# Moving a conversion, three chunks and an output step round the first join of a one-core delta-rule and hard-swish kernel

## The chip, the cores and the metric

The kernel runs on one core of a Trainium2 chip. The metric is the device time of one execution in microseconds (us). The kernel before takes 664.41 us, the median of 3 runs (663.94 to 665.17). A profiled execution of it took 662.06 us, with a span of 660.3 us from its first to its last instruction.

A core has five instruction queues that run side by side and wait for each other by semaphores: PE (matrix multiplication, into PSUM), VectorE (DVE), ScalarE (ACT), GpSimd (POOL) and SyncE (SP), which here issues the loads and stores. Each queue runs its instructions in the order in which the program has them. An instruction that waits holds all that stand behind it on its queue.

## The reference

Two blocks, one behind the other. The first is the delta rule, for 4 batches and 8 heads, 768 steps in time and 48 values a head; the second is a hard-swish MLP on 3072 tokens (384 to 2048 to 384).

```python
k_n = k / (norm(k) + 1e-06)
for t in range(S):
    y[:, :, t] = einsum('bhd,bhde->bhe', q[:, :, t], state)
    v_old = einsum('bhde,bhd->bhe', state, k_n[:, :, t])
    state = state + bt * einsum('bhd,bhe->bhde', k_n[:, :, t], v[:, :, t] - v_old)
...
h = x @ w_in
g = h * clip(h + 3.0, 0.0, 6.0) / 6.0
out = g @ w_out
```

`x` is `y` with its heads put side by side: 3072 rows of 384.

## The kernel before

**Time in chunks.** The 768 steps are cut into N = 24 chunks of C = 32, numbered t. Within a chunk the recurrence is a triangular system of 32 by 32 for each batch and head. `prep` (L505) makes keys, their transposes (`pt`, L524) and the products of keys with keys and queries (`sc`, L547), masked into L and LB (L558). The chunks are inverted in groups: group 0 is chunk 0 alone, group 1 is chunks 1 to 4. `halves_of` (L715) inverts the two 16 by 16 halves of every system of group 1 at once on VectorE: a transpose (L469), then 28 dependent steps that alternate between a product (L730) and a subtraction (L735), a memset (L740) and a transpose back (L473). `join` (L666) puts the halves of one chunk together: a memset on POOL (L691), a transpose on VectorE (L694), a product on PE (`pi`, L684), an addition and a transpose on VectorE (L698, L702), a second product `pi`, and a copy into X on ScalarE (L710). The first join is that of chunk 1.

**The chain.** `chain(t)` (L787) carries the state from chunk to chunk: `ks` (L806) from the state, R on VectorE (L901, L909), `pz` (L827) from X and R, a copy Z on ScalarE (L927), `su` (L938) and the new state (L956). Beside it runs the output of the chunk: `py` (L827's helper, from Z and LB), y (L861 on ScalarE for chunk 0, L843, L819 and L863 for the others), the transposes `yt` (L873) and the copy xT (L877), from which the MLP starts.

**The MLP.** Two chunks make a block of 256 tokens. For block 0, `up(0, 0)` and `up(0, 1)` (L982) run the first matrix for one chunk of tokens each, in 16 pieces of 128 hidden columns, called chunks of `ph` here: three matmuls (L994, 6 records in the trace), a relu on ScalarE (L1001) and a VectorE instruction (L1004) that writes g and frees the PSUM bank. Banks come from a ring of four (`NPM`), which `py`, `yt`, `pi`, `pz` and `pt` use too; a new user takes the bank whose last reader stands earliest in the order, and waits for that reader.

**The weights.** The two matrices come in 16 pieces in a form that has to be converted: four *scale steps* a piece on ScalarE (L356), which write one of two buffers `es[i % 2]` in turn, and three *conversion steps* on VectorE (L378, L383, L389), of which the last reads that buffer and writes the matrix:

```python
d, z = raws[i], like(es[i % 2], i)
...
out=weights[i][0], in0=mf, scalar=2.0**-20, in1=like(es[i % 2], i).bitcast(BF16),
```

Pieces are counted from 0 in the code: the seventh is i = 6, the ninth i = 8, and both use `es[0]`.

**The order.** The first part of the program is written out by hand: the text `ORDER` is read word by word, and each word records the next step of one generator, `*n` times. Behind it a plan goes on by slots. The words that matter here:

- `a`: a scale step. `c`: a conversion step. `w`, `k`, `q`, `v`: one load of weights, keys, queries or values, issued by SP
- `y0`: the steps of the output of chunk 0 (`py`, y, `yt`, xT). `h1`: the steps of chain 1
- `i1`: the steps of `halves_of` for group 1. `x1`, `x2`: the steps of the joins of chunks 1 and 2. `n5`: the norms of keys of chunk 5 (L407 on ScalarE, L413 on VectorE)
- `ua`: the matmuls of one chunk of `ph` of `up(0, 0)`. `ra`: its relu. `ga`: its L1004

Of the kernel before, what the change touches and what calls it, by code (L numbers as in the profile page):

```python
# [23 lines left out]
m0 a n2 m1 p0 x0*2 w q x0 n1 x0*3 c*2 n2 a k s p1*2 a s*2 k q s*2 x0 n2 k*2 c x0 n2 x0 w q a*4 q p1  # L24
n2 k*2 a x0 m2 p1 c*2 p1 n2*3 b1 q b0 s p1 x0 q w x0 n2 q*2 c*3 x0 n4 k p1 k p2*2 x0*2 a*2 c a*2 q*3
a*2 w v p3*2 q x0 q n4 p2*2 c p2 v c n4*2 a*3 z v n4 c a m3 v c p2 n4*2 q p2 k c b2 h0 c h0 w a*2 h0
p4*2 a*2 m4 p3 q*4 h0 q k w p4*2 c*5 v*2 p3 k p3*3 k*2 p4*2 v*2 p4 m6 k a w a w i1*3 k i1*7 a i1*2 a
i1*2 v i1*2 k b3 k y0 c y0*3 ua*2 ra*2 i1*3 w v ga v a*3 i1*2 ua i1 h1 i1 q w ua ra ua i1 ra*2 ga i1
k ua a*2 ra ga i1 ga ua ra ua ra i1 ga i1*4 ua ga n5 x1*2 k x1 c a ra v a*2 ga x2 k*2 ga*2 ua*2 x1
ra*2 x1*2 ua h1*2 n5 k ga c ra ga*2 h1 c y1*2 ua ra w ga ua ra x2 n5 ga y1*2 ua ra ga h1 v*3 n5*2 k  # L30
y1*2 ua a ra x2 ub*2 a n5 rb*2 h1 x3 ga c*2 v W a h2 y2 gb ub rb gb x2 gb ub*2 n5*2 b4 rb n5 x2*2 h2
gb rb gb m5 a n5*2 y2 ub rb gb v c q*2 v q*5 n5 ub n5 rb gb h2 c h2 q ub y2 h2 y2 rb ub p5 b5 rb
gb*2 a*2 x3 p5 ub y2*2 k p5*2 h2 rb h3 p5 gb h3 ub*2 q rb gb rb gb ub a x3 p6 v c x4 x3 rb gb ub p7
rb gb y3 c*2 v c p7*2 y3 v p7*2 b6 x3 q x3 ub p6 h3 a p6 c p5*2 rb gb k m7 w p6 h3 u p6 k*2 q*3 a*2
y3 a p6 c y3 v y3*2 u n9 v k q a c a c*2 u*2 ru gu w k a*2 c a*2 x4 c*2 ru p7 a gu k u a*2 p7 p6 m8
u*3 a k u*2 k h3 w ru*2 a*2 gu*2 x4 c*2 x4 k c*2 a p8 k a*2 u ru k h3 u*2 h4 ru a b8 gu k gu y4 p8*3
u h4 k*2 c q k*9 q u p8*2 x4 k ru k*2 gu k c n9 q u q*2 p8 k*2 b7 n9*2 i2 u x4 q i2*2 q ub ru gu u
rb gb i2*2 h4*2 u*2 i2 ru i2*6 y4 i2 gu i2*7 u i2 ru gu i2 u*3 ru i2*4 gu ru i2*2 v i2 c gu u*3 a u
ru c i2 u*2 i2 gu i2*3 q i2*5 y4 h4 n9 i2 e*2 n9*2 i2*4 q i2 y4 e n9 u ru i2*3 u i2 ru*2 gu h4 u n9
i2*2 u i2 e i2*6 y4 u k n9*3 u gu i2 y4 n9 i2 p9 q i2*2 gu  # L40
"""


# [1521 lines left out]
```

## Time and profile before

| what | value |
|---|---|
| median of 3 runs | 664.41 us |
| the profiled execution | 662.06 us |
| its span | 660.3 us |
| PE busy, 0 to 45 us | 24.69 us |
| PE busy, 47.5 to 61.24 us | 9.81 of 13.74 us |
| VectorE busy, 47.5 to 61.24 us | 12.95 of 13.74 us |
| ScalarE busy, 47.5 to 61.24 us | 10.62 of 13.74 us |
| PE busy, 61.24 to 140 us | 78.76 of 78.76 us |
| PE idle before `yt` of chunk 0, for y (L861) | 2.41 us |
| PE idle before the first `ph`, for xT (L877) | 0.58 us |
| PE idle before the first `pi` of the join | 0.94 us |

Times in the views are in us from the start of the span. In the timeline a line has start, length, engine, line of the code, operation, what is written and read, and how often; idle time before it stands in square brackets. In the table by stretches a line has the stretch, its length, busy time of PE, of PE's weight loads, VectorE, ScalarE and POOL with the number of instructions, then PE's granted clock as a share of full speed, the mean share of the DMA engines, and GB/s. The profile's lines for dependent VectorE instructions overlap at their ends by a little.

### The profile page before, as it was taken

How to read it: one execution, taken by the hardware profiler on the slowest of the kernel's cores; microseconds unless marked ns; L12 is line 12 of the kernel's file. 1: busy time of each engine (PE TensorE's matmuls, PEld its weight loads, DVE VectorE, ACT ScalarE, POOL GpSimd, SP SyncE). 2: the span in 40 equal slices, each digit the busy share in tenths (PEclk: the TensorE clock that was granted, in tenths of full speed). 3: DMA queues.
4: the chain of work that ended last, by engine and by line, in shares of the span. 5: the costliest groups of instructions: out<-in, count | busy, mean ns of one | idle time of the engine just before them, and what ended most of it. 6: DMA issues, size and time to landing. Idle time of an engine off the chain costs nothing.

```text
span 660.3 us, 26640 instructions
## 1 busy us (share of the span) xinstructions
PE 632.5 (96%) x11640; PEld 569.2 (86%) x11640; DVE 499.2 (76%) x1170; ACT 282.3 (43%) x548; POOL 225.1 (34%) x352
## 2 busy tenths in 40 slices
PE   2768999999999999999999999999999999999997
PEld 2658987776689989999999999999999999999997
DVE  5899877798657988758988848979658998456354
ACT  5887689332243154154154244244244144153250
POOL 6531022003661353553254354164051242331430
PEclk9998999999999999999999999999999999999999
DMA  7888346202040030041030030020020020000000
GB/s 174 204 198 235 77 102 164 51 25 43 9 87 18 3 74 3 3 90 22 3 74 3 2 74 3 2 63 2 3 50 2 3 49 3 23 18 2 26 1 24
DMA packets 88692, 33.28 MB, mean 50 GB/s; under 512 B 80224, under 2 KB 83424, under 8 KB 88576
## 3 DMA queue, kind: packets, MB, share of 16 engines
q1 hardware_dynamic: 88224, 31.29, 20.8%
q8 instruction: 91, 1.49, 0.9%
q10 hardware_dynamic: 352, 0.30, 0.2%
q14 instruction: 25, 0.20, 0.1%
HBM read 26.84 MB, written 4.72 MB: 48 GB/s over the span
## 4 chain that ended last, share of the span: by engine, by line
PE 91%; DVE 3%; DMA 2%; SPq 1%; ACT 1%; issue 1%; DVEq 0%
PE po L1226 28%; PE ph L1066 27%; PE ph L994 9%; PE po L1162 6%; PE ks L806 4%; PE su L938 3%; PE pt L524 3%; PE pz L827 3%; PE py L827 3%; PE sc L547 2%; PE yt L873 1%; DMA spare<-in_moe_w_in_dram 1%; PE pi L684 1%; DMA w_out<-in_moe_w_in_dram 1%; SPq L168 1%
## 5 line engine op out<-in xcount | busy, mean ns | idle before, releaser
L1066 PE MATMUL ph<-xT,w_in 128*128 128x128 f32 (+1 forms) x720 | 156.8, 321 | 0.0
L1030 POOL TENSOR_TENSOR g<-g 128x256 f32<-128x256 f32 (+1 forms) x144 | 88.6, 616 | 104.7 <-ACT g L1080 99.1
L1066 PEld LDWEIGHTS ph<-xT,w_in 128*128 128x128 f32 x720 | 116.8, 191 | 6.7
L1226 PE MATMUL po<-w_out,g 128*128 128x192 f32 x640 | 110.6, 326 | 0.0
L1226 PEld LDWEIGHTS po<-w_out,g 128*128 128x128 f32 x640 | 104.6, 190 | 0.5
L1080 ACT ACTIVATE g<-ph 128x512 f32<-128x512 f32 x72 | 43.1, 598 | 105.1 <-PE ph L1066 105.1
L1226 PE MATMUL po<-spare,g 128*128 128x192 f32 x480 | 86.7, 332 | 0.0
L1226 PEld LDWEIGHTS po<-spare,g 128*128 128x128 f32 x480 | 77.2, 190 | 1.8
L994 PE MATMUL ph<-xT,w_in 128*128 128x128 f32 (+1 forms) x384 | 72.0, 338 | 0.6 <-ACT xT L877 0.6
L1236 POOL TENSOR_TENSOR o<-o,u 128x192 f32<-128x192 f32 x18 | 13.3, 739 | 163.8 <-ACT o L1233 86.6
L994 PEld LDWEIGHTS ph<-xT,w_in 128*128 128x128 f32 x384 | 59.6, 195 | 7.7 <-ACT xT L877 0.8
L1093 DVE TENSOR_TENSOR g<-ph,g 128x256 f32<-128x256 f32 x72 | 30.2, 419 | 46.8 <-PE ph L1066 33.5
L759 DVE TENSOR_TENSOR pr<-A 128x30 f32<-128x30 f32 (+9 forms) x150 | 57.3, 382 | 3.3
L1212 DVE TENSOR_TENSOR g<-g 128x512 f32<-128x512 f32 x80 | 56.1, 722 | 3.5 <-PE po L1226 3.5
L1113 DVE SCALAR_TENSOR_TENSOR g<-o,g 128x512 f32<-128x512 f32 x72 | 52.6, 730 | 7.8 <-ACT o L1110 7.7
L764 DVE TENSOR_TENSOR A<-A,pr 128x30 f32<-128x30 f32 (+9 forms) x150 | 55.1, 367 | 3.3
L1110 ACT ACTIVATE o<-g,halves 128x512 f32<-128x512 f32 x72 | 52.2, 725 | 11.3 <-DVE g L1113 8.4
L1066 PE MATMUL ph<-beta_tok,sums_in 128*128 128x128 f32 x288 | 55.9, 275 | 0.0
L356 ACT ACTIVATE spare<-spare,places 128x768 uint16<-128x768 uint16 (+1 forms) x56 | 52.8, 947 | 3.2 <-DMA kf<-in_k_dram 1.6
L1233 ACT ACTIVATE o<-po 128x192 f32<-128x192 f32 x40 | 13.3, 332 | 82.7 <-PE po L1226 79.2
L510 POOL TENSOR_TENSOR kb<-kf,inv 128x384 f32<-128x384 f32 x24 | 21.7, 907 | 75.5 <-issue 43.1
L1162 PE MATMUL po<-w_out,g 128*128 128x384 f32 x128 | 45.4, 490 | 0.0
(141 smaller groups left out, 1019.1 us busy)
## 6 DMA issues: line engine op xcount, KB each, us to landing
kf<-in_k_dram SPq DMA_DIRECT2D x96, 48.0 KB, 2.6
qb<-in_q_dram SPq DMA_DIRECT2D x96, 48.0 KB, 2.4
vf<-in_v_dram SPq DMA_DIRECT2D x96, 48.0 KB, 2.1
out_dram<-o SPq DMA_DIRECT2D x90, 48.0 KB, 1.6
spare<-in_moe_w_in_dram SPq DMA_DIRECT2D x4, 768.0 KB, 6.6
w_out<-in_moe_w_in_dram SPq DMA_DIRECT2D x4, 768.0 KB, 6.1
w_out<-in_moe_w_out_dram SPq DMA_DIRECT2D x4, 768.0 KB, 5.8
spare<-in_moe_w_out_dram SPq DMA_DIRECT2D x4, 768.0 KB, 5.2
```

The source lines that it names most:

```text
L356: nc.scalar.activation(out=z, in_=z if n else d.bitcast(I16)[:, :, :, 3], func=func, bias=places[:, n : n + 1], scale=scale,)
L759: nc.vector.tensor_tensor(out=pv, in0=A[:, j + 1 :, j].unsqueeze(2).to_broadcast([n, w, j]), in1=A[:, j, 0:j].unsqueeze(1).to_broadcast([n ...
L764: nc.vector.tensor_tensor(out=A[:, j + 1 :, 0:j], in0=A[:, j + 1 :, 0:j], in1=pv, op=ALU.subtract)
L994: nc.tensor.matmul(ph[:, cols], lhsT=w_in[:, s, f * 128 : (f + 1) * 128], rhs=xT[:, s, cols], start=(s == 0), stop=(s == NKT - 1),)
L1030: nc.gpsimd.tensor_tensor(out=out, in0=a, in1=b, op=op)
L1066: nc.tensor.matmul(ph[:, n], lhsT=w, rhs=x, start=start, stop=stop, skip_group_check=True)
L1080: nc.scalar.activation(out=gt, in_=ph[:], func=ACTF.Copy)
L1110: nc.scalar.activation(out=r, in_=g, func=ACTF.Relu, bias=half, scale=1.0 / 6.0)
L1113: nc.vector.scalar_tensor_tensor(out=g, in0=r, scalar=1.0, in1=g, op0=ALU.min, op1=ALU.mult)
L1162: nc.tensor.matmul(pos[c][:], lhsT=gs[blk, f // 2][:, f % 2, c * P : (c + 1) * P], rhs=w_out[:, f, :], start=(f == 0), stop=(f == NFC - 1),)
L1212: nc.vector.tensor_tensor(out=A(f, *out, 4), in0=A(f, *a, 4), in1=A(f, *b, 4), op=op)
L1226: nc.tensor.matmul(ps[n][:], lhsT=A(f - f % 2, *a)[:, f % 2], rhs=b[:, f], start=(f == 0), stop=(f == HF - 1),)
```

## The change

Only the text `ORDER` changes. The words are the same 782; those between the 226th and the 337th stand in another order, and from `h1 c y1` on both lists are alike, with the lines broken elsewhere.

```diff
-p4*2 a*2 m4 p3 q*4 h0 q k w p4*2 c*5 v*2 p3 k p3*3 k*2 p4*2 v*2 p4 m6 k a w a w i1*3 k i1*7 a i1*2 a
-i1*2 v i1*2 k b3 k y0 c y0*3 ua*2 ra*2 i1*3 w v ga v a*3 i1*2 ua i1 h1 i1 q w ua ra ua i1 ra*2 ga i1
-k ua a*2 ra ga i1 ga ua ra ua ra i1 ga i1*4 ua ga n5 x1*2 k x1 c a ra v a*2 ga x2 k*2 ga*2 ua*2 x1
-ra*2 x1*2 ua h1*2 n5 k ga c ra ga*2 h1 c y1*2 ua ra w ga ua ra x2 n5 ga y1*2 ua ra ga h1 v*3 n5*2 k
...
+p4*2 a*2 m4 p3 q*4 h0 q k w p4*2 c*5 v*2 p3 k p3*3 k*2 p4*2 v*2 p4 m6 k a w*2 i1 y0*2 a y0*2 i1*2 k
+i1*7 a ua ra i1*2 a ua ra i1*2 ua ga a ra h1 v k b3 k i1 ga i1 a w v*2 ua*2 i1 ga i1 ra*2 i1*2 ua ga
+i1 ra a i1 ua ga i1 q w ra i1 ua ga ra i1 k ua i1 a ga ra i1 ua i1 ga ra i1*2 ua ra ua i1 x1 n5 x1 c
+a ga ra k x1 a v a*2 x2 k*2 ga x1*3 h1 c h1 n5 k c ga*2 h1 c y1*2 ua ra w ga ua ra x2 n5 ga y1*2 ua
+ra ga h1 v*3 n5*2 k y1*2 ua a ra x2 ub*2 a n5 rb*2 h1 x3 ga c*2 v W a h2 y2 gb ub rb gb x2 gb ub*2
...
```

What that makes of each queue:

- **PE**: twelve chunks of `ph` stand ahead of the join's first product, where nine stood. Before, two chunks stood between the join's two products and one between the second product and `pz`; now none does. All else keeps its order.
- **ScalarE**: y of chunk 0 (L861) stands behind the first scale step of the seventh piece instead of behind all four, and xT (L877) behind the second. The scale steps of the seventh and eighth piece alternate with the relus. All relus up to that of the eleventh chunk stand ahead of L407, the first scale step of the ninth piece and the relu of the twelfth chunk; then come the other three scale steps of that piece, L710 and L927. Before, the first scale step of the ninth piece stood ahead of the relus of chunks 6 to 8, the second ahead of that of chunk 9, the other two ahead of those of chunks 10 and 11; then came L710, and behind it the relu of chunk 12.
- **VectorE**: L389 of the seventh piece stood in the elimination of group 1, behind its fifteenth step; now it stands behind L694. Eight L1004 stand in the elimination instead of five, and none between L473 and L694 instead of one. Two stand between L389 and L698; before, L378 of the eighth piece and three L1004 stood between L694 and L698. L378 now stands behind L909.
- **POOL and SP**: the same order of instructions as before.

More of the change, by code (lines that the diff above doesn't have):

```diff
@@ L31 @@
[L31 to L40, printed above, removed]
+p4*2 a*2 m4 p3 q*4 h0 q k w p4*2 c*5 v*2 p3 k p3*3 k*2 p4*2 v*2 p4 m6 k a w*2 i1 y0*2 a y0*2 i1*2 k
@@ new lines @@
+i1*7 a ua ra i1*2 a ua ra i1*2 ua ga a ra h1 v k b3 k i1 ga i1 a w v*2 ua*2 i1 ga i1 ra*2 i1*2 ua ga
+i1 ra a i1 ua ga i1 q w ra i1 ua ga ra i1 k ua i1 a ga ra i1 ua i1 ga ra i1*2 ua ra ua i1 x1 n5 x1 c
+a ga ra k x1 a v a*2 x2 k*2 ga x1*3 h1 c h1 n5 k c ga*2 h1 c y1*2 ua ra w ga ua ra x2 n5 ga y1*2 ua
+ra ga h1 v*3 n5*2 k y1*2 ua a ra x2 ub*2 a n5 rb*2 h1 x3 ga c*2 v W a h2 y2 gb ub rb gb x2 gb ub*2
+n5*2 b4 rb n5 x2*2 h2 gb rb gb m5 a n5*2 y2 ub rb gb v c q*2 v q*5 n5 ub n5 rb gb h2 c h2 q ub y2 h2
@@ new lines @@
+y2 rb ub p5 b5 rb gb*2 a*2 x3 p5 ub y2*2 k p5*2 h2 rb h3 p5 gb h3 ub*2 q rb gb rb gb ub a x3 p6 v c
+x4 x3 rb gb ub p7 rb gb y3 c*2 v c p7*2 y3 v p7*2 b6 x3 q x3 ub p6 h3 a p6 c p5*2 rb gb k m7 w p6 h3
+u p6 k*2 q*3 a*2 y3 a p6 c y3 v y3*2 u n9 v k q a c a c*2 u*2 ru gu w k a*2 c a*2 x4 c*2 ru p7 a gu
+k u a*2 p7 p6 m8 u*3 a k u*2 k h3 w ru*2 a*2 gu*2 x4 c*2 x4 k c*2 a p8 k a*2 u ru k h3 u*2 h4 ru a
+b8 gu k gu y4 p8*3 u h4 k*2 c q k*9 q u p8*2 x4 k ru k*2 gu k c n9 q u q*2 p8 k*2 b7 n9*2 i2 u x4 q
@@ L41 @@
+i2*2 q ub ru gu u rb gb i2*2 h4*2 u*2 i2 ru i2*6 y4 i2 gu i2*7 u i2 ru gu i2 u*3 ru i2*4 gu ru i2*2
+v i2 c gu u*3 a u ru c i2 u*2 i2 gu i2*3 q i2*5 y4 h4 n9 i2 e*2 n9*2 i2*4 q i2 y4 e n9 u ru i2*3 u
+i2 ru*2 gu h4 u n9 i2*2 u i2 e i2*6 y4 u k n9*3 u gu i2 y4 n9 i2 p9 q i2*2 gu
 """
```

## The prediction

> **What bounds the kernel now.** I read first the busy shares, then the chain of waits round the moved work, then the timeline there, then the clock by stretches.
>
> ```profile
> PE 632.5 (96%) x11640; PEld 569.2 (86%) x11640; DVE 499.2 (76%) x1170; ACT 282.3 (43%) x548; POOL 225.1 (34%) x352
> ```
>
> PE is the bound of the whole. From 68.87 us to the end its row in the table by stretches is 588.05 busy of 591.43, and the missing 3.38 are the tail behind its last matmul (656.93 to 660.3). Nothing behind the first join can absorb a delay: what PE loses at 65 us, the kernel loses. The chain of waits shows where that regime begins (start, length, what):
>
> ```profile
> 60.83 0.37 DVE sums_in L694
> 61.20 0.04 issue
> 61.24 0.72 PE pi L684 x54
> 61.97 1.53 PE ph L994 x12
> 63.50 0.66 PE pi L684 x54
> 64.16 0.86 PE ph L994 x6
> 65.02 0.88 PE pz L827 x63
> ```
>
> Until 61.2 the chain is VectorE: the elimination of group 1 (L730, L735), its transpose back (L473) and the join's transpose (L694). Then PE never waits: three chunks of `ph` (18 matmul records) lie between the join's products and `pz`, and cover the answers of VectorE (L698, L702) and of ScalarE (L710). The timeline gives the prices on VectorE:
>
> ```profile
> 53.66 0.27 DVE L730 TENSOR_TENSOR pr<-A 128x112 f32<-128x112 f32 x1
> 53.85 0.95 DVE L389 SCALAR_TENSOR_TENSOR w_in<-spare 128x768 f32<-128x768 f32 x1
> 54.72 0.27 DVE L735 TENSOR_TENSOR A<-A,pr 128x112 f32<-128x112 f32 x1
> ...
> 57.22 0.23 DVE L735 TENSOR_TENSOR A<-A,pr 128x72 f32<-128x72 f32 x1
> 57.36 0.28 DVE L1004 SCALAR_TENSOR_TENSOR g<-g,ph 128x128 f32<-128x128 f32 x1
> 57.56 0.21 DVE L730 TENSOR_TENSOR pr<-A 128x52 f32<-128x52 f32 x1
> ```
>
> and on ScalarE round the join:
>
> ```profile
> 58.63 1.00 ACT L356 ACTIVATE spare<-w_out,places 128x768 uint16<-128x768 int16 x1
> 59.54 0.88 ACT L1001 ACTIVATE g<-ph,halves 128x128 f32<-128x128 f32 x3
> ...
> 60.74 0.45 DVE L694 STREAM_TRANSPOSE sums_in<-X 128x256 f32<-128x256 f32 x1
> 61.11 0.52 DVE L378 TENSOR_SCALAR spare<-spare 128x768 uint32<-128x768 uint32 x1
> ...
> 61.53 0.38 ACT L1001 ACTIVATE g<-ph,halves 128x128 f32<-128x128 f32 x1
> 61.78 1.92 ACT L356 ACTIVATE spare<-spare,places 128x768 uint16<-128x768 uint16 x2
> 63.61 0.61 ACT L1001 ACTIVATE g<-ph,halves 128x128 f32<-128x128 f32 x2
> 64.22 0.28 ACT L710 ACTIVATE X<-pi 128x128 f32<-128x128 f32 x1
> ```
>
> L356 at 58.63 is the first scale step of the ninth piece; its three others follow, and only then stands L710, which `pz` needs. The clock by stretches (length, busy PE, PEld, DVE, ACT, POOL, then PEclk):
>
> ```profile
> 44.98:48.39 3.41, 2.32 (x192) 2.09 (x192) 3.38 (x7) 3.35 (x5) 0.46 (x1) 1.00 0.66 191
> 48.39:51.81 3.42, 1.31 (x9) 1.07 (x10) 3.14 (x9) 1.94 (x4) 1.81 (x5) 1.00 1.01 328
> 51.81:55.22 3.41, 3.41 (x41) 3.19 (x40) 3.14 (x10) 2.20 (x4) 0.00 (x0) 0.50 1.05 286
> ...
> 58.63:62.05 3.42, 2.48 (x80) 2.26 (x80) 3.38 (x8) 3.42 (x9) 0.00 (x0) 1.00 0.79 200
> ```
>
> A stretch in which PE was 38% busy is followed by 3.41 us at half clock; 68% and 73% are not.
>
> **The change, part by part.**
>
> *y and xT of step zero earlier.* L861 and L877 pass three scale steps. `py` ends at 47.51, so L861 runs at 47.56 (0.47), `yt` at 48.08 (0.55), L877 behind one scale step at 48.78 (0.49), and the first `ph` starts near 49.32 instead of 51.05. This only fills PE time that was idle (gaps of 2.41 and 0.58 before `yt` and `ph`): worth 0 on VectorE's chain, and it makes the next part possible. The passed scale steps end near 51.5 instead of 49.5; their reader, the seventh piece's L389, now stands at 60.6.
>
> *Three more chunks ahead of the join.* PE: twelve chunks at 0.67 to 0.77 each (36 records in 4.40 us) and `ks` (1.08) from 49.32, some held by a bank that a `g` frees, end near 59.2: free, with 1.4 us of cover. ScalarE's relus come at least 0.6 us before the `g` that needs them; a scale step (0.97) late by more would hold the elimination by what is above that. VectorE: eight `g` stand in the elimination instead of five. One there costs 0.08: 57.22 to 57.56 is 0.34, against 0.27 for the undisturbed pair at 51.00. So +0.24; the sixth, behind L473, lay in the transpose's latency and cost nothing.
>
> *The conversion behind L694.* 53.66 to 54.72 is 1.06 where neighbours stand 0.31 apart: -0.75 on the elimination. So L694 starts at 60.74 - 0.75 + 0.24 = 60.23. This is the gain. L389 then runs 0.37 behind that start: 60.60 to 61.55 (0.95, the row above). Two things wait for it. First, the join's first product: all four banks are taken by chunks 9 to 12, so it needs the ninth `g`, which stands behind L389 (0.87 later, 61.47, ends 61.75). `pi` starts at 61.80, not 60.73. L698 follows at +0.90, L702 at +0.39 (ends 63.53), the second `pi` at 63.58 ends 64.41; L710 could run at 64.46, R (L901, L909) would be there at 64.80 and `pz` could start at 64.85. Second, and later: the scale steps of the ninth piece write the buffer that L389 reads (`es[i % 2]`, pieces 6 and 8). The first can start only at 61.61, three us later than now, and L710 is queued behind it, a relu and three more scale steps. Start to start: 0.91 (58.63 to 59.54), 0.25 (61.53 to 61.78), 0.97 twice (3.98 for a row of four), 0.84 (61.78 + 0.99 to 63.61): L710 at 65.55, done 65.83, `pz` at 65.88. Now it is 64.95: **+0.93**, with as many chunks done ahead of it as before (12 and 12). Bounds of this term: -0.1 if ScalarE were not the last (64.85), +1.3 if each of the five steps takes 0.07 more. I take +0.93, since every step has a row. Behind `pz` the orders of PE and ScalarE are as before, the queues of SP and POOL are the same throughout, and L378 and L383 of the eighth piece keep over 1 us before their chunk.
>
> *The clock.* No row shows PE's idle time as it will be. From about 59.2 to 65.88 it has only two products of 0.7 us. With the windows of this trace (boundaries at 58.63, 62.05, 65.46, 68.87), 58.63 to 62.05 is about 25% busy, less than the 38% that brought half clock; the next one, at half clock, holds the slowed products, 0.9 + 1.3 us or 65% (the second then ends near 65.4, still ahead of L710's turn). That is too little to bring the clock back: from 17.67 to 21.09 PE was busy 2.87 us, 84%, and yet the four transposes at 23.17 took 1.09 (three at 69.86, at full clock, 0.55), though the clock column has 1.00 so early. So 65.46 to 68.87 is at half clock too, and of it 65.88 to 68.87 is time that PE needs: 2.99 us at half speed lose **1.5**. Bounds: 0 if the clock holds, 3.0 for windows that lie so that PE is half-clocked for most of two behind 65.9. I take 1.5, the windows of this trace.
>
> The Trainium skill ("TensorE: Matmul & The Clock Gate", Part 1) says that the clock falls to half after at least one idle window of about 3.4 us, counted by a free-running window. The window length agrees (3.41 here), but the fall here came after a window 38% busy, whose longest gap was shorter (2.41), so I go by the trace. By the skill's words the sum would end at +0.93, since no gap reaches 3.4 us.
>
> **Sum.** +0.93 + 1.5 = +2.4. The profiled execution took 662.06 (span 660.3 and 1.76 outside), so it would be 664.5; the median of the runs shown, 664.41, lies 2.35 above it, which the same difference turns into **666.8**.
>
> **Rivals.**
> 1. *The wait without the clock* (the skill's rule). ScalarE holds `pz` by 0.93, and PE's clock stays up because the gaps (2.6, 1.1 and 1.5 us) are each shorter than a window: 665.3. For it: 68% busy kept the clock. Against: 38% did not.
> 2. *ScalarE doesn't hold the copy* (the other side). If the steps ahead of L710 run in 4.0 us or less from L694's start instead of 5.3, R decides: `pz` at 64.85, -0.1, 664.3; without the ninth `g` on the way it would be -1.05, 663.4. It decides from L710 at 64.5 or earlier. For it: 0.5 us of gain reach L694 for certain. Against: buffer and queue above.
> 3. *A longer cold spell.* The windows fall so that most of 65.9 to 71 is at half clock: +0.93 + 3.0, 668.3. It is the upper part of my own case.
>
> **How the numbers follow.** Forecast with rival 3: 0.66, from 665.6 to 668.5. Rival 1: 0.16. Rival 2: 0.12. Something unseen: 0.06. About 0.2% (1.3 us) is what a measurement of this kernel can tell from no change, so 663.1 and 665.7 are the borders. Slower: 0.66 + 0.02 = 0.68. Same: 0.16 + 0.08 of rival 2 = 0.24. Faster: 0.04 of rival 2's low end and 0.04 unseen = 0.08. The range 664.5 to 668.6 holds the forecast and rival 1 and leaves out most of rival 2.
>
> **What would show it.** L694 near 60.2; the first `pi` near 61.8 behind a `g`; ScalarE idle from 59.3 to 61.6; L710 near 65.6 directly behind three scale steps; PE idle before `pz` by about 1.5 us; PEclk 0.5 in a stretch that reaches past 65.9. I am wrong if L710 follows the second product at once, if PEclk is 1.00 from 65.5 to 69, or if PE has gaps behind `pz`.

## The result and the profile after

The changed kernel takes 666.73 us (median of 22 runs, 664.56 to 667.99), the kernel before, on the same chip, 664.38 us (22 runs, 661.60 to 667.47). The ratio is 1.0035, with a 95% interval of 1.0025 to 1.0045: slower by some 2.3 us (1.7 to 3.0). The profiled execution took 666.68 us with a span of 664.85 us.

The chain of waits behind the join now looks like this (start, length, what):

```profile
64.89 0.62 DVE R L909
65.51 0.78 DVE spare L378
66.29 0.01 issue
66.30 0.26 ACT X L710
66.56 0.04 issue
66.61 1.50 PE pz L827 x64
68.11 2.86 PE ph L994 x12
```

L710, ScalarE's copy into X, is the last thing that `pz` waits for. What stands ahead of it in the chain must be read with care: L378 is put there as its releaser only because it ended 0.01 us earlier. L710 waits for PE's product alone, and that was done at 65.34. The timeline of ScalarE shows what really stood in front (idle time before an instruction in square brackets):

```profile
60.17 0.51 ACT L407 ACTIVATE sq<-kf 128x384 f32<-128x384 f32 x1
62.39 0.98 ACT L356 ACTIVATE spare<-w_out,places 128x768 uint16<-128x768 int16 x1 [1.71 <-DVE w_in L389]
63.28 0.35 ACT L1001 ACTIVATE g<-ph,halves 128x128 f32<-128x128 f32 x1
63.53 2.86 ACT L356 ACTIVATE spare<-spare,places 128x768 uint16<-128x768 uint16 x3
66.30 0.26 ACT L710 ACTIVATE X<-pi 128x128 f32<-128x128 f32 x1
68.18 0.49 ACT L927 ACTIVATE R<-pz 128x384 f32<-128x384 f32 x1 [1.62 <-PE pz L827]
```

ScalarE stood idle for 1.71 us because the ninth piece's first scale step must wait for L389, which has moved behind L694. Then four scale steps and a relu run back to back, and L710 comes behind them, 0.96 us after its product was there. On PE:

```profile
57.80 2.73 PE L994 MATMUL ph<-xT,w_in 128*128 128x128 f32 x23
62.61 0.72 PE L684 MATMUL pi<-X,sums_in 16*32 16x16 f32 x64 [2.08 <-DVE g L1004]
64.29 1.05 PE L684 MATMUL pi<-X,sums_in 32*32 32x16 f32 x64 [0.95 <-DVE sums_in L702]
66.61 1.50 PE L827 MATMUL pz<-R,X 32*32 32x48 f32 x64 [1.27 <-ACT X L710]
68.04 2.93 PE L994 MATMUL ph<-xT,w_in 128*128 128x128 f32 x12
```

Three gaps (2.08, 0.95 and 1.27 us), and each names another releaser: the ninth `g` (L1004) behind L389, the transpose L702, and L710. The last two lines show the other loss: `pz` takes 1.50 us (before 0.95), the same 12 records of `ph` 2.93 (before 1.60). The table by stretches says why (busy PE, PEld, VectorE, ScalarE, POOL, then PEclk):

```profile
57.42:60.83 3.41, 3.11 (x28) 2.92 (x27) 3.31 (x11) 2.96 (x8) 0.00 (x0) 1.00 1.03 245
60.83:64.24 3.41, 0.72 (x64) 0.63 (x64) 2.63 (x8) 1.84 (x3) 0.00 (x0) 1.00 0.65 226
64.24:67.66 3.42, 2.10 (x117) 1.99 (x121) 3.39 (x7) 2.25 (x4) 2.46 (x4) 0.50 0.31 53
67.66:71.07 3.41, 3.41 (x45) 3.07 (x40) 2.60 (x7) 1.39 (x4) 0.00 (x0) 0.50 0.14 24
71.07:74.48 3.41, 3.41 (x143) 3.17 (x139) 1.59 (x4) 1.59 (x5) 0.00 (x0) 1.00 0.02 5
```

A stretch with PE busy for 0.72 of 3.41 us is followed by two at half clock.

The next table sets marks of the runs side by side: length of the elimination (start of L469 to start of the join's L694), of the join (L694 to the start of `pz`), of what follows (`pz` to the `yt` of chunk 1), and the stretch at half clock nearest the join. All in us, one profiled execution each. The profiled execution of e2 (667.77 us) and that of e5 (672.41) were the shortest of their runs, that of e4 (669.55) the longest. The experiments were timed on three chips, each beside the kernel before: it took 664.27 us beside e1 to e4, 663.90 beside e5 to e8 and 662.73 beside e9, so the ratios are what compares.

| run | L469 to L694 | L694 to `pz` | `pz` to `yt` | half clock | timed, ratio to before (95%) |
|---|---|---|---|---|---|
| before | 13.04 | 4.21 | 4.91 | 51.8 to 55.2 | 1 |
| changed | 12.57 | 5.54 | 6.84 | 64.2 to 71.1 | 1.0035 (1.0025 to 1.0045) |
| e1 | 14.60 | 4.70 | 6.83 | 63.5 to 70.4 | 1.0022 (1.0002 to 1.0042) |
| e2 | 12.96 | 6.72 | 8.87 | 63.3 to 73.5 | 1.0110 (1.0073 to 1.0147) |
| e3 | 14.41 | 3.93 | 7.04 | 64.5 to 71.3 | 1.0023 (1.0004 to 1.0043) |
| e4 | 12.77 | 7.23 | 6.41 | 63.7 to 73.9 | 1.0046 (1.0024 to 1.0069) |
| e5 | 12.95 | 5.43 | 5.28 | none before 104 | 1.0172 (1.0156 to 1.0188) |
| e6 | 12.96 | 4.73 | 5.08 | 51.5 to 54.9 | 0.9994 (0.9980 to 1.0009) |
| e7 | 12.98 | 4.90 | 5.05 | 57.8 to 61.2 | 0.9993 (0.9981 to 1.0004) |
| e8 | 13.00 | 5.53 | 6.89 | 64.3 to 71.2 | one run, 666.76 us |
| e9 | 12.42 | 4.21 | 5.40 | 50.9 to 54.3 | 1.0006 (0.9993 to 1.0019) |

From L469 to the `yt` of chunk 1 the changed kernel takes 24.95 us and the one before 22.16: 2.79 more. The spans differ by 4.54. The rest lies outside the moved work: L469 starts 0.80 later, and behind that `yt` the changed kernel takes 0.96 more (588.02 to the last matmul, against 587.06). The last is no effect of the change: the seven other profiles with no matmuls added take 587.5 to 588.2, e6, e7 and e9 among them, which are as fast as the kernel before when timed. The profile of before lies at the low end of its kernel's runs (662.06, with a median of 664.38).

### The profile page after: what moved, and what is told of

It is laid out like the page before. It is cut to its first block, busy times and chain, and to the rows that moved or that the text cites. A ratio compares the mean times of both kernels' runs of the same rounds, so it can differ in the third digit from the quotient of the medians.

```text
span 664.9 us, 26640 instructions
## 1 busy us (share of the span) xinstructions
PE 632.7 (95%) x11640; PEld 569.4 (86%) x11640; DVE 499.9 (75%) x1170; ACT 280.8 (42%) x548; POOL 225.5 (34%) x352
## 4 chain that ended last, share of the span: by engine, by line
PE 92%; DMA 3%; ACT 2%; SPq 1%; issue 1%; DVE 1%; DVEq 0%
PE po L1226 28%; PE ph L1066 27%; PE ph L994 10%; PE po L1162 6%; PE ks L806 4%; PE pt L524 3%; PE su L938 3%; PE py L827 3%; PE pz L827 3%; PE sc L547 3%; PE yt L873 1%; DMA w_out<-in_moe_w_in_dram 1%; ACT spare L356 1%; DMA kf<-in_k_dram 1%; SPq L168 1%
## 5 line engine op out<-in xcount | busy, mean ns | idle before, releaser
L994 PE MATMUL ph<-xT,w_in 128*128 128x128 f32 (+1 forms) x384 | 71.5, 337 | 1.1 <-ACT xT L877 0.7
L994 PEld LDWEIGHTS ph<-xT,w_in 128*128 128x128 f32 x384 | 59.4, 195 | 8.2 <-ACT xT L877 0.9
```

The costliest lines, as they stand in the source:

```text
L994: nc.tensor.matmul(ph[:, cols], lhsT=w_in[:, s, f * 128 : (f + 1) * 128], rhs=xT[:, s, cols], start=(s == 0), stop=(s == NKT - 1),)
```

## The experiments

### e8: the changed kernel, profiled once more

No edit.

> The changed kernel once more, for a second profile of it. Theory: pz 5.4 to 5.6 us behind L694, PEclk 0.50 for two or three stretches of 3.41 us that begin between 62 and 65; L694 12.4 to 12.7 us behind L469 if PE's clock is up when the first chunks run, 14 to 14.6 if it is still at half then, because eight g then come late for the elimination.

It took 666.76 us. The picture is the same to 0.05 us from L694 on: first `pi` 1.54 us behind L694, L710 5.22, `pz` 5.53, half clock from 64.3 to 71.2. The elimination took 13.00 instead of 12.57, so one profile's elimination is good to some 0.4 us only, and no smaller difference in it is read as an effect below. The trace shows where the 0.43 us came from: PE stood still for 0.72 us within `ks` (0.30 in the first profile, in both cases with no releaser named), the chunks behind it came later by that, and a `g` waited 0.41 us for its relu.

### e1: a buffer of its own for the ninth piece

The changed kernel; the scale steps of piece 8 write a buffer that L389 of piece 6 does not read, so that ScalarE need not wait for it.

```diff
-d, z = raws[i], like(es[i % 2], i)
+d, z = raws[i], like(es[2 if i == 8 else i % 2], i)
...
-in1=like(es[i % 2], i).bitcast(BF16),
+in1=like(es[2 if i == 8 else i % 2], i).bitcast(BF16),
...
+es.append(mlp.tile([128, CB, DM], FP32, name="o", bufs=1)[:, 0].bitcast(U16).rearrange("p (s f) -> p s f", s=NKT))
```

> The changed kernel, but the ninth piece's scale steps write a buffer of their own, so that ScalarE does not wait for L389. Theory (L389 behind L694 holds ScalarE's queue ahead of L710, and PE's first product through the ninth g): L710 follows the second product at once, pz starts about 4.6 us behind L694's start instead of 5.5; the first product still waits for the ninth g, so PE still idles and the clock still falls: about 1.0 less than the changed kernel, 665.7. Rival (PE starves because three chunks were taken from between the join's steps, whatever waits): L710 moves, the time stays at 666.7.

665.58 us (12 runs), ratio 1.0022: by the medians 0.9 us of the 2.3 are gone, but the intervals of e1 and of the change overlap, so the time alone doesn't show it. ScalarE's timeline does:

```profile
60.97 0.97 ACT L356 ACTIVATE o<-w_out,places 128x768 uint16<-128x768 int16 x1
61.85 0.35 ACT L1001 ACTIVATE g<-ph,halves 128x128 f32<-128x128 f32 x1
62.10 2.86 ACT L356 ACTIVATE o<-o,places 128x768 uint16<-128x768 uint16 x3
65.84 0.28 ACT L710 ACTIVATE X<-pi 128x128 f32<-128x128 f32 x1 [0.88 <-PE pi L684]
```

The first scale step follows L407 at once, and L710 now waits for PE's product and runs 0.07 us behind its end (0.96 in the change): the join takes 4.70 us, where 4.6 was expected and the change has 5.54. So the buffer was the cause of 0.84 us, and the prediction's second wait is shown. The clock fell all the same, for 6.8 us. That the elimination took 14.60 was not expected; it is taken up under e3.

### e3: both waits taken away

e1, and the ninth `g` ahead of L389 instead of behind it.

```diff
-x1 n5 x1 c a ga ra k x1 a v a*2 x2 k*2 ga
+x1 n5 x1 ga c a ra k x1 a v a*2 x2 k*2 ga
```

> As the run with the own buffer, and the ninth g stands ahead of L389 instead of behind it, so that neither ScalarE nor PE waits for L389. Theory: the first product 0.7 us behind L694's start instead of 1.5, pz 3.8 behind it instead of 5.5; with L694 0.5 earlier than in the kernel before, pz comes about 0.9 earlier than there. If the clock still falls behind the join 664.5 to 665.0, if it holds 663.4. Rival (chunks taken from between the join's steps): PE still idles as in the changed kernel, 666 or more.

665.72 us, ratio 1.0023. The join does what was expected: first `pi` 0.67 behind L694 (change 1.54), `pz` 3.93 behind it, less than the 4.21 of before. The time is 0.7 us above what was expected. VectorE's lines of L1004 in the elimination show one reason:

```profile
55.18 0.29 DVE L1004 SCALAR_TENSOR_TENSOR g<-g,ph 128x128 f32<-128x128 f32 x1 [0.36 <-ACT g L1001]
57.02 0.29 DVE L1004 SCALAR_TENSOR_TENSOR g<-g,ph 128x128 f32<-128x128 f32 x1 [0.77 <-ACT g L1001]
...
59.44 0.29 DVE L1004 SCALAR_TENSOR_TENSOR g<-g,ph 128x128 f32<-128x128 f32 x1 [0.41 <-ACT g L1001]
```

In this execution, as in e1's, PE was at half clock until 54.3 (53.3 in e1), while the first chunks of `ph` ran. Their relus came late, and each `g` that waited for one held the dependent steps of the elimination behind it: 14.41 us instead of 12.57. The edits of e1 and e3 begin only at the join, so they did not bring the early cold spell; whether the timed executions have it can't be seen. What follows: the changed order puts eight `g` of fresh chunks into the elimination, and so makes it depend on PE's clock before the join.

### e4: the three chunks put back

The changed kernel with chunks 10 and 11 between the two products and chunk 12 ahead of `pz`, as before the change.

```diff
-ga ra i1 ua i1 ga ra i1*2 ua ra ua i1 x1 n5 x1 c a ga ra k x1 a v a*2 x2 k*2 ga x1*3 h1 c h1 n5 k c ga*2 h1 c
+ga ra i1*2 ga i1*3 x1 n5 x1 c a ga k x1 a v a*2 x2 k*2 ua*2 x1 ra*2 ga x1*2 ua h1 c h1 n5 k c ga ra ga h1 c
```

> The changed kernel with the three chunks put back: two between the join's products and one behind the second, with their relus and g; y, xT and L389 stay moved. Theory: the first product no longer waits for a g behind L389 (it takes the sixth chunk's bank) and starts 0.5 us behind L694; ScalarE still waits for L389, so pz still starts 5.3 to 5.5 us behind L694; PE's long idle time now lies ahead of the join (57 to 60.7), so half clock falls where PE waits anyway: 665.0 to 665.8. Rival (the three chunks are the whole loss): 664.4 or less.

666.97 us, ratio 1.0046: not better, and 1.2 us above the top of what was expected. PE's timeline:

```profile
57.76 2.96 PE L994 MATMUL ph<-xT,w_in 128*128 128x128 f32 x25
63.71 1.05 PE L684 MATMUL pi<-X,sums_in 16*32 16x16 f32 x64 [2.99 <-DVE sums_in L694]
64.69 2.93 PE L994 MATMUL ph<-xT,w_in 128*128 128x128 f32 x12
67.55 1.05 PE L684 MATMUL pi<-X,sums_in 32*32 32x16 f32 x64
68.53 1.65 PE L994 MATMUL ph<-xT,w_in 128*128 128x128 f32 x6
70.44 1.50 PE L827 MATMUL pz<-R,X 32*32 32x48 f32 x64 [0.26 <-DVE R L909]
```

With y early and nine chunks, PE runs dry 2.99 us before the join; the clock falls, and now the cover itself runs cold: two chunks between the products take 2.93 us instead of 1.60, so PE, not ScalarE, makes the join 7.23 us long. So it is not enough to put the chunks back: the early y (L861, L877) without more work leaves the hole where the cold clock costs most.

### e2 and e5: PE kept busy, to price the clock

Both give PE work of no use in the gaps: they repeat matmuls already made. e2 makes the twelfth chunk four times and the second product two and a half times; e5 makes the twelfth chunk four times ahead of the join, once more behind the first product and twice behind the second, and has its relu behind L710.

```diff
-for s in range(NKT):
+for s in list(range(NKT)) * (4 if (blk, f, half_of) == (0, 11, 0) else 1):
...
-for h in range(H):
+for h in [*range(H), *range(H), *range(H // 2)] if again else range(H):
```

> The changed kernel, with both waits, but PE's idle time is filled: the matmuls of the twelfth chunk are run four times over and the join's second product two and a half times, into the same banks, with the same values. Theory (half of the loss or more is the clock): L710 and pz stay 5.3 and 5.5 us behind L694's start, to 0.2; the granted clock stays at 1.00 behind the join; 1.5 to 2.0 less than the changed kernel, 664.7 to 665.2. Rival (the wait alone is the loss, the clock is a side show): 666.7, no change.

e2 missed: 670.78 us, ratio 1.011. PE waited 0.95 us for the transpose of the join, and from 62.77 us it stood still for 1.00 us with no releaser named. The stretches:

```profile
59.90:63.30 3.40, 1.83 (x150) 1.44 (x148) 2.62 (x9) 3.24 (x5) 1.40 (x3) 1.00 0.17 64
63.30:66.70 3.40, 2.56 (x127) 2.29 (x128) 3.17 (x6) 0.97 (x2) 1.06 (x2) 0.50 0.43 77
```

1.83 of 3.40 us busy did not hold the clock, and it stayed at half for 10.2 us. Some 0.53 us of the pause lie in the first stretch; without them PE would have been busy for 69% of it (an estimate from these rows). So e2 prices nothing. e5, whose edit is (with the relu `ra` moved behind `x1*3`):

```diff
+            for _ in range({"pi1": 1, "pi2": 2}[name] if t == 1 else 0):
+                again[0]()
...
+            mms()
+            if (blk, f, half_of) == (0, 11, 0):
+                again.append(mms)
+                for _ in range(3):
+                    mms()
```

> The changed kernel with both waits, with PE kept busy by full-width matmuls: those of the twelfth chunk are run four times ahead of the join, once more behind its first product and twice behind its second (same bank, same values; its relu stands behind L710 instead of ahead of the scale steps). Theory (the clock falls after a stretch of 3.41 us in which PE is busy less than some 55%, and that costs about 1.9): PEclk 1.00 from the join on, pz 5.2 to 5.5 us behind L694's start as in the changed kernel, 664.5 to 665.0. Rival (the wait alone is the loss): 666.5 to 667.

In the join e5 does what was expected: no gap over 0.1 us, and the clock at 1.00 until 104 us (its lines are numbered differently: L997 is L994, L829 is L827, L940 is L938).

```profile
61.46 0.73 PE L684 MATMUL pi<-X,sums_in 16*32 16x16 f32 x64
62.12 0.94 PE L997 MATMUL ph<-xT,w_in 128*128 128x128 f32 x6
63.14 0.73 PE L684 MATMUL pi<-X,sums_in 32*32 32x16 f32 x64
63.80 1.60 PE L997 MATMUL ph<-xT,w_in 128*128 128x128 f32 x12
65.35 0.88 PE L829 MATMUL pz<-R,X 32*32 32x48 f32 x64
66.16 1.60 PE L997 MATMUL ph<-xT,w_in 128*128 128x128 f32 x12
```

From `pz` to `yt` it takes 5.28 us where the change takes 6.84, with the same instructions. So 1.56 us of the change's loss is the cold clock, priced by itself. The time as a whole missed: 674.82 us, ratio 1.0172, some 10 us over. In the profiled execution (672.41 us) 6.1 us lie in PE's waits from 70 us on:

```profile
PE sc L547 <- issue: 2.9, 2, 2.5
PE py L829 <- issue: 1.6, 1, 1.6
PE su L940 <- issue: 1.6, 1, 1.6
```

The matmuls added lie at 58 to 65 us, the long pauses end at 84.7, 103.6 and 358.6:

```profile
84.70 0.35 PE L940 MATMUL su<-R,bkb 32*64 32x48 f32 x13 [1.58 <-issue]
103.62 0.44 PE L547 MATMUL sc<-KQ 64*32 64x64 f32 x27 [2.46 <-issue]
```

The profile names no releaser for them, but its DMA packets tell what ended them. Each of the three ends 1.3 to 1.5 us behind a 16 KB packet of DMA queue q8, the one that carries PE's instructions (they landed at 83.37, 102.11 and 357.30). The last section has the whole count. So e5 prices the clock round the join, and its time as a whole holds another cost, seen in this size only where matmuls were added.

### e6: the conversion alone

The kernel before, with L389 behind L694, a `g` on either side of it, and the buffer of e1. y, xT and the chunks stay where they were.

```diff
-y0 c y0*3 ua*2 ra*2 ... ga n5 x1*2 k x1 c a ra v a*2 ga x2 k*2 ga*2 ua*2 x1 ra*2 x1*2 ua h1*2 n5 k ga c ra ga*2 h1 c
+y0*4 ua*2 ra*2 ... ga n5 x1*2 ga c ga k x1 a ra v a*2 x2 k*2 ua*2 x1 ra*2 x1*2 ua h1 c ga h1 n5 k ga c ra ga*2 h1 c
```

> The kernel before, with one part of the change in a form that holds nobody: L389 of the seventh piece out of the elimination to behind L694, with one g ahead of it and one behind; the ninth piece's scale steps have a buffer of their own; chunks, y and xT as before. Theory: L694 starts 12.3 us behind L469 instead of 13.0, pz 4.1 to 4.2 behind L694, clock as before: 0.7 to 0.8 less than before, 663.6. Rival (behind L694 the conversion always costs what it saves): 664.4 or more, with pz 5 behind L694.

663.46 us, ratio 0.9994: no difference that the runs can tell, though the interval holds the 0.7 us that was expected too. The gain of 0.75 us on the elimination did not appear in full: 12.96 where 12.3 was expected. VectorE's lines:

```profile
56.69 0.29 DVE L1004 SCALAR_TENSOR_TENSOR g<-g,ph 128x128 f32<-128x128 f32 x1 [0.23 <-ACT g L1001]
56.90 0.21 DVE L735 TENSOR_TENSOR A<-A,pr 128x52 f32<-128x52 f32 x1
57.36 0.29 DVE L1004 SCALAR_TENSOR_TENSOR g<-g,ph 128x128 f32<-128x128 f32 x1 [0.26 <-ACT g L1001]
```

Without L389 the steps run ahead of the relus, and two `g` wait for them: L389 had hidden that they are late. The join then takes 4.73, since the twelfth chunk waits 0.39 us for the bank that L710 frees.

### e7: y and xT early alone

The kernel before, with only the first part of the change.

```diff
-m6 k a w a w i1*3 k i1*7 a ... b3 k y0 c y0*3 ua*2
+m6 k a w*2 i1 y0*2 a y0*2 i1*2 k i1*7 a ... b3 k c ua*2
```

> The kernel before, with only y and xT of step zero ahead of the scale steps (L861 behind the first, L877 behind the second); chunks, relus, g and L389 as before. Theory: the first ph starts 1.3 to 1.7 earlier against L469, the banks then hold PE for the first g, and L694 and pz stay where they were: 664.4, within 0.4. Rival (the early start takes PE's cold time out of the stage and is a gain): 663 or less.

663.30 us, ratio 0.9993: no difference in time, as expected, but not for want of an effect. The first `ph` starts 1.31 us behind L469 instead of 3.35, PE then waits 2.19 and 0.57 us for banks, and the stretches move:

```profile
54.30:57.80 3.50, 1.60 (x11) 1.41 (x12) 3.29 (x17) 1.27 (x4) 0.00 (x0) 0.99 0.85 234
57.80:61.20 3.40, 3.40 (x18) 3.40 (x17) 3.33 (x9) 1.83 (x5) 0.00 (x0) 0.50 0.93 187
```

The idle time that stood ahead of `yt` stands now in the middle of the chunks, and the cold spell comes six us later than before, next to the join: the first `pi` starts 1.17 us behind L694 (0.50 before), since PE is still busy with the slowed chunks. `pz` comes 0.63 us later against L469 (17.88 and 17.25), where it was expected to stay.

### e9: an attempt to keep the gain

e6, with two `g` of the elimination one and two steps later, the twelfth chunk's bank freed ahead of R, and the last scale step of the ninth piece behind L710.

```diff
-ra ga i1 ga ua ra ua ra i1 ga i1*4 ua ga n5 x1*2 ga c ga k x1 a ra v a*2 x2 k*2 ua*2 x1 ra*2 x1*2 ua h1 c ga h1
+ra ga i1 ua ra i1 ga ua ra i1*2 ga i1*2 ua ga n5 x1*2 ga c ga k x1 a ra v a x2 k*2 ua*2 x1 ra*2 ga x1*2 a ua h1 c h1
```

> e6 (before, with L389 behind L694 and the ninth piece's scale steps in a buffer of their own) with three more moves: two of the five g of the elimination one or two steps later, so that they come behind their relus (in e6 they waited 0.23 and 0.26 us); the g that frees the bank of the twelfth chunk ahead of R, not behind L378 (PE waited 0.39); the last scale step of the ninth piece behind L710. Theory (the gain of the conversion is real, and it reaches pz only if the queues of PE and ScalarE keep up): L469 to L694 12.4 to 12.5 (e6 12.96, before 13.04), L694 to pz 4.1 to 4.4 (e6 4.73, before 4.21), PE idle nowhere for more than 0.5 us behind 50.5 but before the first pi (at most 0.8), clock as before; time 663.0 to 663.5, which is 0.7 to 1.2 less than the kernel before where e6 was equal to it. Rival (the conversion's 0.75 us is not to be had, since PE's nine chunks set the end of the elimination): the ninth chunk ends at or behind L694's end, pz as in e6, 663.5 to 664.4.

The marks come as the theory said: elimination 12.42, join 4.21, so `pz` stands 16.63 us behind L469 and not 17.25. The time does not: 663.06 us beside 662.73 for the kernel before, ratio 1.0006 (0.9993 to 1.0019). PE's timeline behind `pz`:

```profile
63.70 1.17 PE L827 MATMUL pz<-R,X 32*32 32x48 f32 x64
64.79 1.88 PE L994 MATMUL ph<-xT,w_in 128*128 128x128 f32 x12
...
72.21 0.72 PE L994 MATMUL ph<-xT,w_in 128*128 128x128 f32 x5 [0.26 <-issue]
```

`pz` takes 0.22 more than before, the 12 records 0.28 more, and at 72.2 there is a pause of 0.26 with no releaser named; the clock is at 1.00 throughout. By the `yt` of chunk 2 the kernel stands 36.44 us behind L469, the one before 36.16: in this execution the 0.62 us were given back within 20 us. The pause of 0.26, and a step of 0.22 within `pz`, end 1.5 and 1.4 us behind a packet of PE's instructions, as in e5; what slows the 12 records stays open. No version tried beats the kernel before.

## Why the prediction was right

**The gain on VectorE.** Forecast: 0.51 off the elimination. Measured 0.47 in the first profile, 0.04 in the second: the sign is right, the size lies within what two executions differ by. The prediction gave the relus at least 0.6 us of margin; a pause of PE in the second profile used it up, and a `g` waited. The step that counted L389 as 0.75 us of pure delay left out what it covered: in e6, with it gone, two waits for relus took 0.49 of it back, and only e9, with its `g` rearranged, kept 0.62.

**y and xT early at nothing.** Right in time (e7), and it brings the chunks forward for the next part: in e6, without it, two `g` wait for their relus (no run has the twelve chunks without it). But it moves PE's idle time toward the join, and with it the cold spell (e4, e7); the prediction saw the idle time and not that.

**Three more chunks free on PE.** They were expected to end 11.5 us behind L469 and ended 12.03 behind it, still ahead of L694's answer. They were not free behind it: with both waits gone, in e3, PE was busy for only 1.59 of the 3.42 us from 61.08, and the clock fell all the same. The prediction has this price, but under the clock. e4 shows that putting them back with y early is no better.

**The two waits on L389.** Forecast from L694 to the first `pi` 1.57, to L710 5.32, to `pz` 5.65; measured 1.54, 5.23, 5.54. From L469 to `pz` the forecast was +0.93 and the profile has +0.86. e1 took the second wait away and got 0.84 us of the join back, which leaves rival 2 (ScalarE doesn't hold the copy) without ground; e3 took both away. One step was added up wrong: a second product that starts at 63.58 and takes 0.73 ends at 64.31, not 64.41. The forecast doesn't rest on it, since R, later than that, set the 64.85.

**The clock.** Forecast +1.5, from one half-clocked stretch that reaches 3 us past `pz`. Measured +1.93 from `pz` to `yt`, and 1.56 by e5, which has the same instructions warm. The windows lay so that the spell reached 4.5 us past the start of `pz`: between the forecast and rival 3. The fall came behind a stretch in which no gap was longer than 2.08 us. The Trainium skill ("TensorE: Matmul & The Clock Gate", Part 1) has the clock fall after at least one idle window of about 3.4 us; the traces do not agree, since a window 21% busy in the change and one 54% busy in e2 (1.83 of 3.40) were enough. Rival 1, which was that rule, fell with it.

**The sum.** +2.4 was forecast; +2.3 (1.7 to 3.0) is measured, and the two terms by the profile are +0.86 and +1.93, +2.79 in one execution; in e8 they are +1.28 and +1.98, 3.26. So the direction and both terms are shown, but that the forecast median of 666.8 and the measured 666.73 lie so close is in part luck: the marks of both profiles come to more than the times do (2.35 by the medians), and what makes up for it is open. No run has the time of the kernel before with the change's order and both terms gone (in e3 the clock still fell, in e5 other pauses came), so that the two terms are the whole difference is read from the marks, not from the times. The signs named ahead were there: L694 earlier against L469 (hardly so in e8), the first `pi` behind a `g`, ScalarE idle, L710 behind the scale steps, PE idle 1.27 us before `pz` (1.5 forecast), half clock past it.

## What to carry to other kernels

Before an instruction is moved behind a long chain, look up who waits for it on the other engines: here its gain of half a microsecond at most on VectorE was paid for with 0.84 us by a buffer that two pieces shared and a queue in which a late step stood ahead of an urgent one. Then add up how busy the matrix engine stays in each window of 3.4 us: work moved ahead of a wait fills one window and empties the next, and the empty one is paid for in the window behind it. And an instruction that looks like pure delay on a chain may be what gives others time to arrive; take it away alone, in an experiment, before its length is counted as a gain.

## What the runs showed of the hardware

- **Where the clock falls.** Over the windows of the eleven profiles from the first recorded change of the clock up to 80 us, each 3.41 us long and laid from the recorded changes of the clock, the full clock fell behind every window in which PE's records were busy for 55% or less (14% to 55%) and held behind every one with 56% or more, matmuls on small tiles counted like others. The way back up has no such border: a window busy from end to end always brought it, but of those 80% to 98% busy some did and some did not (e4 stayed at half behind 98% and 92%, the change rose behind 80% at 47.2).
- **The releaser that the chain names can be a neighbour in time.** In the change it put L378 (ended 66.29) in front of L710 (66.30); in e1 L710 ran at 65.84 while L378 lasted from 65.86 to 66.71.
- **PE's pauses with no releaser follow a load of its instructions.** The trace lists DMA packets of 16 KB of the kind instruction on queue q8. The kernel before has 91 of them for its 11640 matmuls and as many weight loads, which comes to 64 bytes for each (packets, MB, share):

```profile
q8 instruction: 91, 1.49, 0.9%
```

With more matmuls, in e2 and e5, there are 92. Behind 48 us the eleven profiles have 26 pauses of PE over 0.15 us for which no releaser is named (none of them in the kernel before), and every one ends 1.24 to 1.60 us behind the landing of such a packet. They fall on the same places in the row of matmuls: behind the 984th record in five profiles and behind the 2384th in six, in e5 too, where other work stands there. So what PE waited for, as far as these rows tell, is its next instructions. Behind 70 us these pauses were 0.5 us or less in the kernels with as many matmuls as before, and up to 1.0 us in e2 and 2.5 in e5, where matmuls had been added at 58 to 65 us. Why a packet comes in time in one execution and late in another stays open.
